# A decode block on one core: one ring of 160 KB for all loads, in which a load waits only for the readers of the bytes it replaces

## The chip, the cores and the metric

One Trainium2 chip, one of its cores. The metric is device microseconds of one execution, as the median of the fast runs; lower is better. A profile is one such execution with the hardware profiler on; its span is the time between its first and last instruction, and the time of a run is about 1.8 us longer than its span.

## The reference

One decode step of a transformer block, for a batch of 2, with one new token each:

```python
mod = (silu(c) @ w_mod)                    # w_mod 1024 x 6144: six vectors sa, ca, ga, sb, cb, gb
h = layernorm(x) * (1 + ca) + sa
q = h @ wq                                 # 32 heads of 128, 4 key/value heads, 8 query heads share one
p = softmax(q k_cache^T / sqrt(128))       # caches: 2 x 4 x 32768 x 128 each
x = x + ga * (p v_cache) @ wo
h = layernorm(x) * (1 + cb) + sb
x = x + gb * (gelu(layernorm(h) @ w1 + b1) @ w2 + b2)   # w1 1024 x 3584, w2 3584 x 1024
```

All inputs are bf16. K and V are 134.2 MB, the weights 44.0 MB, and each byte is used once for at most 8 query heads: 178.27 MB must come from HBM.

## The kernel before

All loads go out from SP, in one fixed order, into six slots of 16 KB per partition ("ring") and two fixed regions of 32 KB for `wo` and most of `w1`. A load waits for the readers of its slot, and for the load that landed in it last. A K or V chunk is 8192 rows: 16 KB per partition, 2 MB.

```python
seq = [Item("WMODH", 0, nslots=2)] + [Item("WQ", k) for k in range(KT8)]
seq += kv("K", 0) + kv("K", 1) + kv("V", 0)                     # kv: four chunks each
seq += [Item("MODB", 0), Item("MODB", 1)] + kv("K", 2) + kv("V", 1)
# ... (MODB: 1 MB in a slot of 2 MB; WO quarters go to the fixed regions)
seq += kv("K", 7) + kv("V", 6)
seq += [Item("W1", k, fixed="AB") for k in range(4)] + kv("V", 7) + [Item("W1", k, fixed="AB") for k in range(4, 6)]
seq += [Item("W1", k) for k in range(6, KT8)] + [Item("W2", j) for j in range(4)]
# ...
        if it.kind == "WO":                                      # rows of 2 KB
            return A_wo[r0:r0 + 512, :].rearrange("(t p) n -> p t n", p=128)
        if it.kind == "W2":                                      # rows of 2 KB
            return B_w2[it.i * 896:(it.i + 1) * 896, :].rearrange("(k p) n -> p k n", p=128)
```

Per (batch, group) `i` the engines do a whole K pass (64 PE transposes and 64 score matmuls a chunk, eight at a time, the transposed keys copied out of PSUM by DVE or ACT), then a whole V pass for the group before:

```python
    for i in range(1, NBG):
        QK(i)
        softmax_m1(i)
        softmax_back(i - 1)
        # ... (MODB)
        PV(i - 1)                 # per chunk 64 matmuls of 8 columns, V as stationary operand
        # ... (WO_mm: 256 matmuls of one column per batch)
        softmax_aux(i)            # maximum, then eight exponentials on ACT
    # ... last PV, WO, layernorm, W1, GELU, W2, store
```

It leaves out the second of the reference's last two layernorms; the changed kernel has it.

Of the kernel before, what the change touches and what calls it, by code (L numbers as in the profile page):

```python
# [5 lines left out]
ACT = mybir.ActivationFunctionType  # L6
# [6 lines left out]
HQ = 32  # L13
# [6 lines left out]
CH_ROWS = 8192  # L20
TPC = CH_ROWS // 128
NCH = S // CH_ROWS
# [6 lines left out]
R = 6  # L29
NKT = 8  # L30
PIPE = 3
NPKT = 4
NPS = 1
EVAC_PATTERN = ("dve", "act", "dve", "act", "dve", "dve", "act", "dve")
SLOT_BYTES = 16 * 1024


class Tracker:
# [115 lines left out]
    def dma(self, E, fn, key, reads=(), writes=()):  # L154
        self.dma_key(key)
        reads, writes = self._excl(reads, writes)
        waits = self._compute_waits(E, self._dep_tokens(E, reads, writes))
        self.dma_cnt[key] += 16
        token = (key, ("g", len(self.dma_groups[key])))
        self.ops[E].append(("dma", waits, fn, key))  # L160
        self._record(token, reads, writes)
        return token
# [34 lines left out]
def bass_adaLN_cond__gqa_block_cached__mixer_channel_mlp__decode_kernel(  # L197
# [17 lines left out]
    ident = nc.alloc_sbuf_tensor("ident", [128, 128], BF16)  # L215
    identf = nc.alloc_sbuf_tensor("identf", [128, 128], FP32)
    onesf = nc.alloc_sbuf_tensor("onesf", [128, 128], FP32)
    x16 = nc.alloc_sbuf_tensor("x16", [16, 128], BF16)
    c16 = nc.alloc_sbuf_tensor("c16", [16, 128], BF16)
    b1m = nc.alloc_sbuf_tensor("b1m", [FT, 128], BF16)  # L220
    b2m = nc.alloc_sbuf_tensor("b2m", [KT8, 128], BF16)
    smallT = nc.alloc_sbuf_tensor("smallT", [128, 68], FP32)
    xT = smallT[:, 0:16].rearrange("p (b k) -> p b k", b=2)
    cT = smallT[:, 16:32].rearrange("p (b k) -> p b k", b=2)
    b1T = smallT[:, 32:60]
    b2T = smallT[:, 60:68]
    sgT = nc.alloc_sbuf_tensor("sgT", [128, 2, KT8], FP32)
    siluT = nc.alloc_sbuf_tensor("siluT", [128, 2, KT8], BF16)
    stat = nc.alloc_sbuf_tensor("stat", [128, 8], FP32)
    mean = nc.alloc_sbuf_tensor("mean", [128, 2], FP32)  # L230
    rstd = nc.alloc_sbuf_tensor("rstd", [128, 2], FP32)
    xc = nc.alloc_sbuf_tensor("xc", [128, 2, KT8], FP32)
    sq = nc.alloc_sbuf_tensor("sq", [128, 2, KT8], FP32)
    t1 = nc.alloc_sbuf_tensor("t1", [128, 2, KT8], FP32)
    hT = nc.alloc_sbuf_tensor("hT", [128, 2, KT8], BF16)
    modT = nc.alloc_sbuf_tensor("modT", [128, NMOD, 2], FP32)
    qacc = nc.alloc_sbuf_tensor("qacc", [128, 2 * HQ], FP32)
    qT = nc.alloc_sbuf_tensor("qT", [128, 2, HQ], BF16)
    attnT = nc.alloc_sbuf_tensor("attnT", [128, 2, HQ], BF16)
    yT = nc.alloc_sbuf_tensor("yT", [128, 2, KT8], FP32)  # L240
    x1T = nc.alloc_sbuf_tensor("x1T", [128, 2, KT8], FP32)
    h2T = nc.alloc_sbuf_tensor("h2T", [128, 2, KT8], BF16)
    zT = nc.alloc_sbuf_tensor("zT", [128, FT, 2], FP32)
    z2 = nc.alloc_sbuf_tensor("z2", [128, FT, 2], FP32)
    z3 = nc.alloc_sbuf_tensor("z3", [128, FT, 2], FP32)
    th = nc.alloc_sbuf_tensor("th", [128, FT, 2], FP32)
    gT = nc.alloc_sbuf_tensor("gT", [128, FT, 2], BF16)
    mT = nc.alloc_sbuf_tensor("mT", [128, KT8, 2], FP32)
    resT = nc.alloc_sbuf_tensor("resT", [128, 2, KT8], FP32)
    res_bf = nc.alloc_sbuf_tensor("res_bf", [128, 16], BF16)  # L250
    res16 = nc.alloc_sbuf_tensor("res16", [16, 128], BF16)
    m1 = [nc.alloc_sbuf_tensor(f"m1_{i}", [128, HPG], FP32) for i in range(2)]
    gm = [nc.alloc_sbuf_tensor(f"gm_{i}", [HPG, 1], FP32) for i in range(2)]
    diag = [nc.alloc_sbuf_tensor(f"diag_{i}", [HPG, HPG], FP32) for i in range(2)]
    negm = [nc.alloc_sbuf_tensor(f"negm_{i}", [128, HPG], FP32) for i in range(2)]
    rowsum = [nc.alloc_sbuf_tensor(f"rowsum_{i}", [128, HPG], FP32) for i in range(2)]
    rinv = [nc.alloc_sbuf_tensor(f"rinv_{i}", [128, HPG], FP32) for i in range(2)]

    KB = 1024
    ARENA = R * SLOT_BYTES + 32 * KB + 32 * KB + 32 * KB  # L260
    arena = nc.alloc_sbuf_tensor("arena", [128, ARENA], mybir.dt.uint8)
    abase = nc.lookup_mloc(arena).addr

    def at(name, shape, dtype, off):
        return nc.alloc_sbuf_tensor_at(name, list(shape), dtype, offset=abase + off)

    def slot_off(sl):
        return sl * SLOT_BYTES

    slots = [at(f"slot{i}", [128, SLOT_BYTES // 2], BF16, slot_off(i)) for i in range(R)]  # L270
    regA = R * SLOT_BYTES
    regB = regA + 32 * KB
    regC = regB + 32 * KB
    wo_blk = [at("wo0", [128, 16, DM], BF16, regA), at("wo1", [128, 16, DM], BF16, regB)]
    w1p = [at(f"w1p{k}", [128, F], BF16, (regA + k * 7 * KB) if k < 4 else (regB + (k - 4) * 7 * KB)) for k in range(6)]
    for i in range(2):
        for q in range(4):
            T.interval(f"wo{i}q{q}", (regA if i == 0 else regB) + q * 8 * KB, (regA if i == 0 else regB) + (q + 1) * 8 * KB)
    for k in range(6):
        off = (regA + k * 7 * KB) if k < 4 else (regB + (k - 4) * 7 * KB)  # L280
        T.interval(f"w1p{k}", off, off + 7 * KB)
    S_sb = at("S_sb", [128, HPG, NCH * TPC], FP32, regC)
    E_sb = [at(f"E_sb{i}", [128, HPG, NCH * TPC], BF16, regC + 8 * KB + i * 4 * KB) for i in range(2)]
    KT_sb = [at(f"KT_sb{i}", [128, 8, 128], BF16, regC + 16 * KB + i * 2 * KB) for i in range(NKT)]
    assert 16 + 2 * NKT <= 32

    psKT = [nc.alloc_psum_tensor(f"psKT{i}", [128, 1024], BF16) for i in range(NPKT)]
    psS = [nc.alloc_psum_tensor(f"psS{i}", [128, 512], FP32) for i in range(NPS)]
    psO = nc.alloc_psum_tensor("psO", [128, 512], FP32)
    psM = nc.alloc_psum_tensor("psM", [128, 512], FP32)  # L290
    psX = nc.alloc_psum_tensor("psX", [128, 512], FP32)

    T.inst("pool", lambda e: e.memset(ident[:, :], 0.0), writes=["ident"])
    T.inst("pool", lambda e: e.affine_select(out=ident[:, :], in_=ident[:, :], compare_op=ALU.not_equal, fill=1.0,
                                             base=0, pattern=[[-1, 128]], channel_multiplier=1), reads=["ident"], writes=["ident"])
    T.inst("pool", lambda e: e.memset(identf[:, :], 0.0), writes=["identf"])
    T.inst("pool", lambda e: e.affine_select(out=identf[:, :], in_=identf[:, :], compare_op=ALU.not_equal, fill=1.0,
                                             base=0, pattern=[[-1, 128]], channel_multiplier=1), reads=["identf"], writes=["identf"])
    T.inst("pool", lambda e: e.memset(onesf[:, :], 1.0), writes=["onesf"])

    T.dma("act", lambda e: e.dma_start(x16[:, :], A_x.rearrange("b o (k p) -> (b o k) p", p=128)), key="ld", writes=["x16"])
    T.dma("act", lambda e: e.dma_start(c16[:, :], c.rearrange("b (k p) -> (b k) p", p=128)), key="ld", writes=["c16"])
    T.dma("act", lambda e: e.dma_start(b1m[:, :], B_b1.rearrange("(f p) -> f p", p=128)), key="ld", writes=["b1m"])
    T.dma("act", lambda e: e.dma_start(b2m[:, :], B_b2.rearrange("(f p) -> f p", p=128)), key="ld", writes=["b2m"])

    class Item:
        def __init__(self, kind, i=0, cc=0, nslots=1, fixed=None):
            self.kind, self.i, self.cc, self.nslots, self.fixed = kind, i, cc, nslots, fixed
            self.pos = None
            self.view = None  # L310
            self.regions = None
            self.issued = False

    def kv(kind, i):
        return [Item(kind, i, cc) for cc in range(NCH)]

    def woq(i, qs):
        return [Item("WO", i, q, fixed="AB") for q in qs]
    K4 = kv("K", 4)
    V3 = kv("V", 3)  # L320
    seq = [Item("WMODH", 0, nslots=2)] + [Item("WQ", k) for k in range(KT8)]
    seq += kv("K", 0) + kv("K", 1) + kv("V", 0)
    seq += [Item("MODB", 0), Item("MODB", 1)] + kv("K", 2) + kv("V", 1)
    seq += [Item("MODB", 2), Item("MODB", 3)] + kv("K", 3) + kv("V", 2)
    seq += [Item("MODB", 4), Item("MODB", 5)] + woq(0, [0, 1]) + K4[0:2] + woq(0, [2, 3]) + K4[2:4]
    seq += [Item("MODB", 6), Item("MODB", 7)] + woq(1, [0, 1]) + V3[0:2] + woq(1, [2, 3]) + V3[2:4]
    seq += kv("K", 5) + kv("V", 4)
    seq += kv("K", 6) + kv("V", 5)
    seq += kv("K", 7) + kv("V", 6)
    seq += [Item("W1", k, fixed="AB") for k in range(4)] + kv("V", 7) + [Item("W1", k, fixed="AB") for k in range(4, 6)]  # L330
    seq += [Item("W1", k) for k in range(6, KT8)] + [Item("W2", j) for j in range(4)]
    lookup = {}
# [405 lines left out]
```

## Time and profile before

| | before |
|---|---|
| time, median of 3 runs | 448.21 us (446.92 to 448.82) |
| span of the profile | 445.5 us |
| PE, ACT, DVE busy | 69%, 32%, 35% |
| bytes from HBM, mean rate | 178.28 MB, 400 GB/s over the span |

These lines are from the page of the kernel before. They give the busy tenths of the 16 DMA engines, and what they moved, in 40 slices of 11.1 us; then two DMA queues (loads, and instruction fetches): packets, MB, time taken as a share of 16 engines; then the chain of work that ended last, by engine.

```profile
DMA  8999999999999999999999999999999999999990
GB/s 316 421 425 433 419 423 431 420 344 424 425 430 420 427 427 419 414 413 410 417 413 403 428 425 430 422 384 415 430 424 418 427 382 383 427 425 414 394 369 34
...
q1 hardware_dynamic: 21616, 178.27, 96.7%
q8 instruction: 61, 1.00, 0.9%
...
PE 52%; DMA 19%; issue 11%; ACT 9%; SPq 6%; DVE 3%; ACTq 0%; DVEq 0%
```

The DMA engines are busy nearly everywhere, so the load stream is near its limit, yet several slices move clearly less than the 425 to 433 of the best. And the chain that ended last is mostly PE, with 11% of "issue", which is time in which an engine waited for nothing that the profile shows. In order of time, the last load in this chain, and the piece after it (start, us, what):

```profile
239.86 18.71 DMA slot_54<-in_A_v_cache_dram
258.62 1.89 PE psO L595 x64
```

Up to 258.6 us PE (106 us) and the loads (84 us) take turns in the chain. After that no load is in it: of its last 187 us, 125 are PE, 33 "issue" and 18 ACT. So the stream was not the limit from end to end. In the last part the computation ended last, and the loads waited for it to free their slots.

The next view is the busy time by stretch (microseconds from the start of the span; the last two columns are the share of the DMA engines and the rate):

```profile
core 0: us, PE busy (x) PEld busy (x) DVE busy (x) ACT busy (x) POOL busy (x), PEclk, DMA share, GB/s
30.00:88.00 58.00, 44.87 (x957) 43.34 (x958) 28.36 (x44) 26.80 (x41) 0.00 (x0) 0.94 1.01 426
88.00:104.00 16.00, 12.76 (x378) 12.32 (x376) 6.55 (x9) 5.07 (x6) 0.00 (x0) 0.86 0.94 368
184.00:248.00 64.00, 37.95 (x910) 35.97 (x906) 19.07 (x32) 16.89 (x30) 0.00 (x0) 0.69 1.02 411
...
360.00:378.00 18.00, 16.24 (x372) 16.01 (x370) 10.97 (x17) 10.79 (x19) 0.00 (x0) 0.93 0.94 373
408.00:430.00 22.00, 13.77 (x460) 13.32 (x457) 3.73 (x22) 1.76 (x3) 0.00 (x0) 0.50 1.03 396
```

There are two kinds of loss. In 88 to 104 and 360 to 378 the DMA engines are partly idle (shares 0.94): holes. In 184 to 248 and 408 to 430 they are fully busy and slow: these are the stretches of `wo` and `w2`, read in rows of 2 KB. Compared with 427 GB/s I work out, from the rates of each microsecond, 5.9 us lost in holes (2.2 in 88 to 104, 1.4 in 288 to 306, 2.2 in 360 to 378) and 3.9 in the slow stretches (2.4 and 1.5).

What SP waited for (us in total, times, longest), then PE's longest "issue" entry (time in which an engine waited for nothing that the profile shows):

```profile
SPq L184 <- PE psKT L540: 194.6, 28, 18.0
SPq L184 <- PE psO L595: 77.3, 24, 9.8
...
PE psO L595 <- issue: 23.8, 12, 2.6
```

```profile
82.87 0.33 SPq L396 DMA_DIRECT2D slot_52<-in_A_v_cache_dram  x1
88.67 0.33 SPq L396 DMA_DIRECT2D modb_83<-in_w_mod_dram  x1
94.46 0.33 SPq L396 DMA_DIRECT2D modb_84<-in_w_mod_dram  x1
97.60 0.33 SPq L396 DMA_DIRECT2D slot_49<-in_A_k_cache_dram  x1
```

SP issues whenever PE has read a slot out, once in 5.8 us in a K pass. At 427 GB/s (my estimate from the rate above) a full slot of 2 MB takes 4.9 us to load, but in 88.67 and 94.46 the next item of the fixed order is `modb`, 1 MB: half a slot, 2.5 us of work for the DMA engines each.

PE's "issue" gaps come above all in PV. Often PE runs 128 of its matmuls, which with their weight loads are 256 instructions, in 3.6 us, and then stands still for 2.3 to 2.6 us. Two of these gaps begin at 140.4 and 146.3, as a fetch of 16 KB of instructions starts (140.3 and 146.4), and end 1.3 to 1.5 us after its 1.05 us. It looks as if PE waited for its next instructions, but no run tests that.

At the end, PE's timeline (start, us, instruction, count, idle before and what ended it):

```profile
434.13 1.15 PE L689 MATMUL psM<-gT,w2v_93 128*128 128x2 bf16 x38 [1.97 <-DVE mT L680]
...
440.14 1.63 PE L689 MATMUL psX<-gT,w2v_96 128*128 128x2 bf16 x56
443.09 0.28 PE L699 MATMUL psM<-ident,res_bf 128*16 128x128 bf16 x1 [1.32 <-DVE res_bf L698]
```

The 224 matmuls of `w2` start at 434.1, when GELU is done, and run until 441.8.

### The profile page before, as it was taken

To read this page: it belongs to the slowest core of one execution; us is meant where nothing else is said; L and a number is where in the kernel's file an instruction comes from. 1 tells how busy PE (TensorE), PEld (TensorE's weight loads), DVE (VectorE), ACT (ScalarE), POOL (GpSimd) and SP (SyncE) were. 2 spreads that over 40 slices of the span, in tenths; PEclk is the share of its full clock that TensorE was granted. 3 is DMA by queue.
4 is the path that set the end of the run, shared out by engine and by line. 5 is a ranking of instruction groups with operands and counts; after the bars stand their busy time and mean duration, and the time that the engine had idled before them with its cause. 6 is when DMAs were issued, how large, how long until landed. Compare 5 with 4: busy or idle time off the path is not lost.

```text
span 445.5 us, 16705 instructions
## 1 busy us (share of the span) xinstructions
PE 309.0 (69%) x7805; PEld 295.2 (66%) x7805; DVE 157.9 (35%) x294; ACT 143.3 (32%) x251; POOL 1.3 (0%) x9
## 2 busy tenths in 40 slices
PE   1445987996986698638684258887977698755555
PEld 1445877895986598638574158886976588744455
DVE  1101656551652265215351004551643065400221
ACT  2001556630751166024250004640752065305100
POOL 1000000000000000000000000000000000000000
PEclk9999996995996599657696555995896579855555
DMA  8999999999999999999999999999999999999990
GB/s 316 421 425 433 419 423 431 420 344 424 425 430 420 427 427 419 414 413 410 417 413 403 428 425 430 422 384 415 430 424 418 427 382 383 427 425 414 394 369 34
DMA packets 21807, 179.35 MB, mean 403 GB/s; under 512 B 1770, under 2 KB 1770, under 8 KB 11498
## 3 DMA queue, kind: packets, MB, share of 16 engines
q1 hardware_dynamic: 21616, 178.27, 96.7%
q8 instruction: 61, 1.00, 0.9%
q14 instruction: 8, 0.07, 0.0%
q10 hardware_dynamic: 122, 0.02, 0.0%
HBM read 178.28 MB, written 0.00 MB: 400 GB/s over the span
## 4 chain that ended last, share of the span: by engine, by line
PE 52%; DMA 19%; issue 11%; ACT 9%; SPq 6%; DVE 3%; ACTq 0%; DVEq 0%
PE psKT L540 23%; PE psO L595 10%; DMA slot_53<-in_A_k_cache_dram 10%; PE psS L520 8%; SPq L396 5%; DMA wqv_77<-in_A_wq_dram 5%; DMA slot_54<-in_A_v_cache_dram 4%; PE psM L607 3%; ACT KT_sb_67 L550 3%; ACT S_sb L525 3%; ACT KT_sb_72 L550 2%; ACT E_sb_65 L576 1%; PE psM L572 1%; PE psM L478 1%; PE psM L567 1%
## 5 line engine op out<-in xcount | busy, mean ns | idle before, releaser
L550 ACT ACTIVATE KT_sb_72<-psKT 128x1024 bf16<-128x1024 bf16 x32 | 32.7, 1023 | 44.7 <-PE psKT L540 44.7
L550 ACT ACTIVATE KT_sb_67<-psKT 128x1024 bf16<-128x1024 bf16 x25 | 25.6, 1024 | 58.1 <-PE psKT L540 58.1
L576 ACT ACTIVATE E_sb_64<-S_sb,negm 128x256 bf16<-128x256 f32 x32 | 16.2, 506 | 78.1 <-DVE negm L574 77.3
L540 PE MATMUL psKT<-ident,slot_53 128*128 128x128 bf16 x384 | 35.5, 255 | 8.2 <-DMA slot_53<-in_A_k_cache_dram 8.2
L576 ACT ACTIVATE E_sb_65<-S_sb,negm 128x256 bf16<-128x256 f32 x32 | 16.2, 506 | 61.8 <-DVE negm L574 61.0
L553 DVE COPY KT_sb_70<-psKT 128x1024 bf16<-128x1024 bf16 x32 | 22.1, 692 | 36.2 <-PE psKT L540 36.2
L540 PEld LDWEIGHTS psKT<-ident,slot_53 128*128 128x128 bf16 x384 | 28.7, 116 | 8.4 <-DMA slot_53<-in_A_k_cache_dram 8.3
L540 PE MATMUL psKT<-ident,slot_51 128*128 128x128 bf16 x320 | 28.5, 251 | 4.7 <-DMA slot_51<-in_A_k_cache_dram 4.7
L540 PE MATMUL psKT<-ident,slot_54 128*128 128x128 bf16 x384 | 29.3, 218 | 1.2 <-issue 1.2
L598 DVE TENSOR_TENSOR attnT<-psO,rinv 128x8 bf16<-128x8 f32 x8 | 1.3, 167 | 79.2 <-PE psO L595 79.2
L553 DVE COPY KT_sb_66<-psKT 128x1024 bf16<-128x1024 bf16 x32 | 22.1, 692 | 19.6 <-PE psKT L540 19.4
L553 DVE COPY KT_sb_73<-psKT 128x1024 bf16<-128x1024 bf16 x32 | 22.1, 692 | 19.3 <-PE psKT L540 19.3
L553 DVE COPY KT_sb_68<-psKT 128x1024 bf16<-128x1024 bf16 x32 | 22.1, 692 | 17.9 <-PE psKT L540 17.9
L540 PE MATMUL psKT<-ident,slot_49 128*128 128x128 bf16 x320 | 27.0, 240 | 1.3 <-issue 1.3
L540 PEld LDWEIGHTS psKT<-ident,slot_51 128*128 128x128 bf16 x320 | 23.3, 114 | 5.4 <-DMA slot_51<-in_A_k_cache_dram 4.8
L550 ACT ACTIVATE KT_sb_69<-psKT 128x1024 bf16<-128x1024 bf16 x25 | 25.7, 1028 | 3.3 <-PE psKT L540 3.3
L540 PE MATMUL psKT<-ident,slot_50 128*128 128x128 bf16 x320 | 24.4, 218 | 0.3 <-issue 0.3
L540 PE MATMUL psKT<-ident,slot_52 128*128 128x128 bf16 x320 | 24.3, 218 | 0.0
L540 PEld LDWEIGHTS psKT<-ident,slot_49 128*128 128x128 bf16 x320 | 21.6, 108 | 1.4 <-issue 1.4
L553 DVE COPY KT_sb_71<-psKT 128x1024 bf16<-128x1024 bf16 x32 | 22.1, 691 | 1.0 <-PE psKT L540 0.8
L540 PEld LDWEIGHTS psKT<-ident,slot_54 128*128 128x128 bf16 x384 | 21.8, 97 | 0.0
L525 ACT ACTIVATE S_sb<-psS 128x512 f32<-128x512 f32 x32 | 19.0, 593 | 7.9 <-PE psS L520 7.9
(195 smaller groups left out, 517.1 us busy)
## 6 DMA issues: line engine op xcount, KB each, us to landing
slot_53<-in_A_k_cache_dram SPq DMA_DIRECT2D x6, 2048.0 KB, 15.6
slot_54<-in_A_k_cache_dram SPq DMA_DIRECT2D x6, 2048.0 KB, 17.6
slot_51<-in_A_v_cache_dram SPq DMA_DIRECT2D x6, 2048.0 KB, 17.1
slot_52<-in_A_v_cache_dram SPq DMA_DIRECT2D x6, 2048.0 KB, 19.8
slot_49<-in_A_k_cache_dram SPq DMA_DIRECT2D x5, 2048.0 KB, 17.1
slot_50<-in_A_k_cache_dram SPq DMA_DIRECT2D x5, 2048.0 KB, 20.3
slot_51<-in_A_k_cache_dram SPq DMA_DIRECT2D x5, 2048.0 KB, 19.2
slot_52<-in_A_k_cache_dram SPq DMA_DIRECT2D x5, 2048.0 KB, 19.2
```

What stands on the lines that cost most here:

```text
L396: T.dma("sp", lambda e, dst=dst, src=src: e.dma_start(dst, src), key=key, writes=list(it.regions))
L478: T.inst("pe", lambda e, jc=jc: e.matmul(psM[:, 288 + jc * 2:290 + jc * 2], lhsT=wv[:, jc * 128:(jc + 1) * 128], rhs=siluT[:, :, kb], star ...
L520: T.inst("pe", lambda e, sbk=sbk, sp=sp, kn=kn, jj=jj: e.matmul(psS[sbk][:, sp * HPG:(sp + 1) * HPG], lhsT=KT_sb[kn][:, jj, :], rhs=qT[:, ...
L525: T.inst("act", lambda e, sbk=sbk, col0=col0: e.activation(S_sb[:, :, col0:col0 + 64], psS[sbk][:, 0:512].rearrange("p (t h) -> p h t", h= ...
L540: T.inst("pe", lambda e, kq=kq, jj=jj, sl_view=sl_view, t=t: e.transpose(psKT[kq][:, jj * 128:(jj + 1) * 128], sl_view[:, t * 128:(t + 1) ...
L550: T.inst("act", lambda e, kq=kq, kn=kn: e.activation(KT_sb[kn][:, :, :], psKT[kq][:, 0:1024].rearrange("p (a n) -> p a n", a=8), ACT.Copy) ...
L553: T.inst("dve", lambda e, kq=kq, kn=kn: e.tensor_copy(KT_sb[kn][:, :, :], psKT[kq][:, 0:1024].rearrange("p (a n) -> p a n", a=8)), reads=[ ...
L567: T.inst("pe", lambda e: e.matmul(psM[0:HPG, 0:128], lhsT=m1[j][:, :], rhs=identf[:, :], start=True, stop=True), reads=[f"m1_{j}", "identf ...
L572: T.inst("pe", lambda e: e.matmul(psM[:, 128:128 + HPG], lhsT=onesf[0:HPG, :], rhs=diag[j][:, :], start=True, stop=True), reads=["onesf", ...
L576: T.inst("act", lambda e, h=h: e.activation(E_sb[j][:, h, :], S_sb[:, h, :], ACT.Exp, bias=negm[j][:, h:h + 1], scale=SCALE, accum_out=row ...
L595: T.inst("pe", lambda e, t=t, sl_view=sl_view, tg=tg: e.matmul(psO[:, 0:HPG], lhsT=sl_view[:, t * 128:(t + 1) * 128], rhs=E_sb[j][:, :, tg ...
L607: T.inst("pe", lambda e, wv=wv, t=t, cch=cch: e.matmul(psM[:, col0 + cch:col0 + cch + 1], lhsT=wv[:, t % 16, cch * 128:(cch + 1) * 128], r ...
```

## The change

One ring of 160 KB per partition for everything. Every load has its own semaphore and waits for one thing, the PE count at which the readers of the bytes under it are done. K chunk n alternates with V chunk n-5. `w_mod` comes whole at the start, in rows of 12 KB, and no longer in half filled slots between the caches. `w1` and `w2` come last (before, four of the eight blocks of `w1` came ahead of the last V pass), `wo` and `w2` are laid out so that rows are 16 KB and 8 KB. PV takes E as the stationary operand (32 columns) and 512 columns of V as the moving one, four matmuls to four column groups; so 16 instead of 64 per chunk. The maximum is taken per chunk, S is double-buffered as E already was, and the softmax steps are put between the groups of the next K chunk. The core of the diff:

```diff
-R = 6
-NKT = 8
+VLAG = 5
+NKT = 6
+RING = 160 * 1024
-SLOT_BYTES = 16 * 1024
@@ class Tracker
-    def dma(self, E, fn, key, reads=(), writes=()):
+    def dma(self, E, fn, key, reads=(), writes=(), frees=()):
         self.dma_key(key)
         reads, writes = self._excl(reads, writes)
-        waits = self._compute_waits(E, self._dep_tokens(E, reads, writes))
+        tokens = self._dep_tokens(E, reads, writes)
+        for r in frees:
+            reg = self._region(r)
+            assert reg[1], r
+            tokens.extend(reg[1])
+        waits = self._compute_waits(E, tokens)
@@ stream (the old slots, regions and seq are gone; cut)
+    for n in range(NK + VLAG):
+        if n < NK:
+            add(("K", n), [TPC, D], kv_src(A_k_cache, n // NCH, n % NCH))
+        v = n - VLAG
+        if v >= 0:
+            add(("V", v), [TPC, D], kv_src(A_v_cache, v // NCH, v % NCH))
+            if v % (2 * NCH) == 2 * NCH - 1:
+                g = v // (2 * NCH)
+                add(("wo", g), [8, DM], A_wo[g * 1024:(g + 1) * 1024, :].rearrange("(p j) n -> p j n", j=8))
+    # (then w1 in 4 items, w2 in 4 items)
+    w2_v = B_w2.rearrange("(q p j) n -> p q (j n)", p=128, j=4)
+    def need(*key):
+        it = by_key[key]
+        while pos[0] <= it.n:
+            cur = stream[pos[0]]
+            old = [o.reg for o in stream[:cur.n] if o.off < cur.off + cur.nbytes and cur.off < o.off + o.nbytes]
+            # ... dst, the view of cur
+            T.dma("sp", lambda e, dst=dst, src=cur.src: e.dma_start(dst, src), key=f"d_{cur.reg}", writes=[cur.reg], frees=old)
+            pos[0] += 1
+        return it
@@ PV
-            for t in range(TPC):
-                tg = cc * TPC + t
-                T.inst("pe", ... matmul(psO[:, 0:HPG], lhsT=sl_view[:, t * 128:(t + 1) * 128], rhs=E_sb[j][:, :, tg], ...
+        for t4 in range(TPC // 4):
+            tg = cc * TPC + t4 * 4
+            q = t4 % 4
+            pe(... matmul(psO[32 * q:32 * q + 32, :], lhsT=E_sb[j][:, tg // 4, :, :].rearrange("p h t -> p (h t)"),
+                          rhs=it.view[:, t4 * 4:t4 * 4 + 4, :].rearrange("p t d -> p (t d)"), ...
```

The intent: no load waits for anything but free space, PE may fall far behind before the stream stops, and the tail of the computation runs while the last weights load.

## The prediction

> **What bounds the kernel now.** The load stream. The page counts 178.27 MB on the SP queue; the 16 DMA engines are busy 96.7% of a 445.5 us span for it, at a mean 403 GB/s; PE is busy 69%, ACT 32%, DVE 35%. In the busy table by 11 us stretches, undisturbed K and V stretches move 422 to 430 GB/s. [...]no stretch passes 434. At 425 the bytes alone take 419.5 us. So 26 us of the span can be won at most:
> - start: first bytes at 2.3 us (kept);
> - holes: 262 GB/s at 93-96 us, 336 at 99-102, 306 to 393 at 363-375, a dip at 297-308. SP waits for slots with unread K or V (waits of the SP queue: 195 us on transposes, 77 on PV). By subtraction about 9 us of stream time;
> - short rows: w2 and wo are read in 2 KB runs and move at 386 to 400 GB/s with the DMA engines fully busy. For 15.7 MB that costs about 3.4 us against 425;
> - tail: the last byte lands near 434.3 us. Of the 11 us after it 8 are the w2 product (224 small matmuls that begin only after GELU, at 434, with an issue gap), 3.7 the closing chain and store.
>
> **What the change does.** Six 16 KB slots plus fixed regions become one ring of 160 KB, ten chunks. A load waits for one PE count, the readers of the chunk ten places earlier. A chunk takes 4.9 us at 425 GB/s, so PE may fall some 35 us behind before the stream stops; before, about 20, with whole K passes alternating with whole V passes, where now K n and V n-5 alternate. wo and w2 rows become 16 and 8 KB. PV turns from 64 matmuls of 8 columns per chunk into 16 of 512 columns in four column groups. The tail gains a layernorm (about 3.5 us in the chain of waits).
>
> **Does PE keep up?** In the timeline a K chunk with its scores takes 5.8 us at full clock. PV is estimated: 8192 columns, against 8 transposes of 128 columns in 0.5 us, so at most 3.9 us if the four groups run serially, about 1 if they overlap. Together 6.8 to 9.7 us per step, against 9.9 us of loading. ACT (3 evictions of 1.02, a score copy of 0.59, two exponentials of 0.5) needs about 5 us, DVE about 4.5. The stream stays the limit, narrowly if PV serialises.
>
> **Tail.** After the last V chunk, wo, w1 and w2 (16.8 MB, 39 us) still stream, and fit in the ring. Last PV, extraction, wo, two layernorms, w1 and GELU take about 27 us, so they hide; 32 matmuls (about 1 us) and the closing chain of 3.7 us follow the last byte. That saves about 6 us.
>
> **Sum.** Span: 2.3 start + 1 ramp + 418 (426 GB/s) + 5 tail = 426; timed runs exceed the span by 2.7 us: **429 us**, range 424 to 437. Chances: faster by over 2% 0.91, within 2% 0.08, slower 0.01.
>
> **What would show it.** DMA row at 9 in every slice, at least 420 GB/s through K/V and over w2; SP's waits for PE remaining but harmless; last byte about 5 us before the end; PE waiting for K and V chunks; w1 done before w2 lands.
>
> **What would make it wrong.** PV serial at a low granted clock, so that PE needs over 9.9 us per step (PE busy above 9 tenths, DMA holes between chunks); softmax stalls longer than the ring covers; w1 starting late, so w2 queues behind it; more loads outstanding slowing each other below 420 GB/s.

The sum: 2.3 + 1 + 418 + 5 is 426, and with 2.7 it is 429. The 426 GB/s in it are from the stretches of the kernel before (422 to 430).

## More of the kernel before

From the trace's record of arriving semaphore increments, the last load landed at 436.9. So 8.6 us of the span came after the last byte. But `w2` did not wait for it: its matmuls waited for GELU, whose chain is the computation since 258.6.

## The result, and the profile after

| | before | after |
|---|---|---|
| time, median of 4 runs each | 447.56 us (445.39 to 448.82) | 431.44 us (431.30 to 431.47) |
| span of the profile | 445.5 us | 429.7 us |
| last byte landed | 436.9 us | 425.7 us |
| from there to the end | 8.6 us | 4.0 us |
| instruction fetches of 16 KB | 61 | 47 |

The ratio is 0.9642 (95% interval 0.9604 to 0.9680). Ratios here are the mean time of one kernel's fast runs over the mean of the other's of the same rounds, so not quite the ratio of the medians. The change saves 15.8 us of span: the last byte lands 11.2 us earlier (436.9 less 425.7), and 4.6 us less follow it. For the kernel before this split is bookkeeping, as its end did not wait for its last byte.

The same lines of the page of the changed kernel, with one more ahead of them, the busy us of the engines (share of the span, number of instructions):

```profile
PE 292.2 (68%) x6035; PEld 258.2 (60%) x6035; DVE 162.5 (38%) x344; ACT 158.9 (37%) x266; POOL 1.3 (0%) x9
...
DMA  8999999999999999999999999999999999999992
GB/s 332 432 422 426 433 432 424 432 424 427 427 432 427 426 433 429 427 433 426 426 432 426 430 433 424 429 432 426 429 429 428 430 429 424 435 424 424 427 386 112
...
q1 hardware_dynamic: 14112, 178.27, 97.6%
q8 instruction: 47, 0.77, 0.6%
...
DMA 70%; PE 24%; ACT 2%; DVE 2%; issue 1%; SPq 1%; ACTq 0%
```

From the second slice to the second but last no slice is under 420 GB/s, and the chain that ended last is now 70% DMA, where it was 52% PE. The stretches shown above for the kernel before, here in the changed kernel:

```profile
30.00:88.00 58.00, 38.15 (x948) 37.06 (x948) 19.91 (x35) 15.86 (x18) 0.00 (x0) 1.00 1.01 427
88.00:104.00 16.00, 10.99 (x218) 10.02 (x219) 5.89 (x13) 11.14 (x23) 0.00 (x0) 0.89 1.01 429
184.00:248.00 64.00, 49.71 (x973) 43.48 (x970) 30.68 (x57) 32.25 (x57) 0.00 (x0) 0.89 1.01 429
...
360.00:378.00 18.00, 9.84 (x128) 4.91 (x124) 5.39 (x17) 7.71 (x19) 0.00 (x0) 0.70 1.00 427
408.00:430.00 22.00, 9.83 (x312) 9.23 (x311) 1.55 (x7) 0.25 (x1) 0.00 (x0) 0.50 0.59 247
```

The K/V stage runs at 427 to 431 GB/s. What SP waited for:

```profile
SPq L344 <- PE psS L441: 197.4, 31, 11.3
SPq L344 <- PE psM L510: 47.1, 3, 16.3
SPq L344 <- PE psO L473: 36.1, 27, 8.0
```

SP still waits 281 us for PE in these three lines, where it was 272 in the two before. That means nothing by itself: it waits with up to ten loads in flight (K and V loads land 43 to 44 us after their issue, by the page), and the DMA queue is not empty meanwhile. The wait of SP, which runs ahead, is not a loss here: the DMA row stays at 9 tenths from the second slice to the last but one.

A step of PE at full clock (the last group of a K chunk, the 16 PV matmuls, and the next K chunk), from the timeline:

```profile
307.44 0.34 PE L441 MATMUL psS<-qT,KT_sb 128*128 128x8 bf16 x8
307.72 1.05 PE L473 MATMUL psO<-V,E_sb 128*32 128x512 bf16 x16
312.09 0.62 PE L546 MATMUL psKT<-ident,K 128*128 128x128 bf16 x8 [3.33 <-DMA K<-in_A_k_cache_dram]
```

PV takes 1.0 us, then PE sits idle for 3.3 us until the next K chunk lands. (At full clock a step is 6.2 us, eight groups of 0.65 us and PV. At lower clock it is longer: in 184 to 248, at a mean granted clock of 0.89, PE was busy for 49.7 of 64 us.) The tail:

```profile
423.31 1.87 PE L591 MATMUL psS<-gT,w 128*128 128x2 bf16 x64 [3.28 <-DMA w<-in_B_w_dram]
425.74 1.01 PE L591 MATMUL psS<-gT,w 128*128 128x2 bf16 x32 [0.56 <-DMA w<-in_B_w_dram]
427.28 0.28 PE L597 MATMUL psM<-ident,res_bf 128*16 128x128 bf16 x1 [0.53 <-DVE res_bf L596]
```

`w2` is now used as it lands, and only 32 matmuls and the closing chain come after the last byte at 425.7.

One stretch does not fit: 408 to 430 moves only 247 GB/s. Reading it by the microsecond, the DMA share is 1.0 until 416, and from 418 to 424 it is 0.4 to 0.5: as if half of the DMA engines had nothing left while the other half still work. The trace records when each of the 16 increments of a load's semaphore arrived, but not from which of the 16 DMA engines. I read them as one from each engine, which fits the DMA share (0.5 from 419 to 420, when 8 of the last load's 16 have arrived). I print some loads of the changed kernel, in us:

```
load of               first   8th    9th    last   spread
wmod, 5th              21.1   21.3   21.4   21.5    0.4
wmod, 6th              24.8   25.0   25.0   26.3    1.6
a chunk near  88       85.7   86.1   87.2   88.7    3.0
a chunk near 148      144.1  145.2  147.0  148.5    4.4
a chunk near 218      212.2  214.3  216.4  218.0    5.8
a chunk near 287      280.2  282.2  285.9  287.5    7.3
a chunk near 361      353.2  356.0  360.2  361.8    8.6
w2, the last          416.7  419.5  423.7  425.7    9.0
```

PE takes up the last load with its last increment (425.74 in the timeline above, for 425.7), so the stream ends when the latest engine ends: 425.7, where the first was done at 416.7. The spread hardly creeps, it jumps by 1.1 to 1.3 us at six loads, the ones shown first landing late at 26.3, 88.7, 148.5, 218.0, 287.5 and 361.8. The instruction fetches number 1, 9, 17, 25, 33 and 41 start at 21.3, 86.3, 142.4, 214.9, 285.0 and 356.9. So the spread grows once in eight fetches, just after a fetch. That is a theory to test: fetches of 16 KB (one packet each, 0.94 us in the mean of 47) fall in turn on the same eight engines and make these late.

### The profile page after: what moved, and what is told of

The parts are those of the page before. It is cut to its first block, busy times and chain, and to the rows that moved or that the text cites. A ratio compares the mean times of both kernels' runs of the same rounds, so it can differ in the third digit from the quotient of the medians.

```text
span 429.7 us, 12974 instructions
## 1 busy us (share of the span) xinstructions
PE 292.2 (68%) x6035; PEld 258.2 (60%) x6035; DVE 162.5 (38%) x344; ACT 158.9 (37%) x266; POOL 1.3 (0%) x9
## 4 chain that ended last, share of the span: by engine, by line
DMA 70%; PE 24%; ACT 2%; DVE 2%; issue 1%; SPq 1%; ACTq 0%
DMA K<-in_A_k_cache_dram 50%; PE psKT L546 15%; DMA V<-in_A_v_cache_dram 9%; DMA w<-in_B_w_dram 7%; DMA wmod<-in_w_mod_dram 5%; PE psS L441 4%; PE psO L473 2%; PE psM L510 1%; ACT E_sb L462 1%; SPq L344 1%; PE psM L494 0%; DVE KT_sb L552 0%; PE psM L483 0%; ACT L462 0%; DVE msum L488 0%
## 5 line engine op out<-in xcount | busy, mean ns | idle before, releaser
L546 PE MATMUL psKT<-ident,K 128*128 128x128 bf16 x2048 | 181.1, 240 | 55.1 <-DMA K<-in_A_k_cache_dram 54.2
L546 PEld LDWEIGHTS psKT<-ident,K 128*128 128x128 bf16 x2048 | 138.2, 108 | 70.0 <-DMA K<-in_A_k_cache_dram 63.5
L550 ACT ACTIVATE KT_sb<-psKT 128x1024 bf16<-128x1024 bf16 x96 | 98.3, 1024 | 190.2 <-PE psKT L546 181.3
L552 DVE COPY KT_sb<-psKT 128x1024 bf16<-128x1024 bf16 x160 | 108.2, 689 | 137.7 <-PE psKT L546 137.0
L441 PE MATMUL psS<-qT,KT_sb 128*128 128x8 bf16 x2048 | 91.6, 168 | 7.2 <-ACT KT_sb L550 4.5
L441 PEld LDWEIGHTS psS<-qT,KT_sb 128*128 128x128 bf16 x2048 | 84.0, 100 | 8.6 <-ACT KT_sb L550 4.9
L473 PE MATMUL psO<-V,E_sb 128*32 128x512 bf16 x512 | 38.2, 424 | 10.1 <-DMA V<-in_A_v_cache_dram 9.5
L462 ACT ACTIVATE E_sb<-S_sb,negm 128x256 bf16<-128x256 f32 x64 | 32.5, 508 | 7.0 <-DVE negm L460 5.2
L447 DVE TENSOR_REDUCE m1c<-S_sb 128x8 f32<-128x512 f32 x32 | 22.0, 688 | 14.1 <-ACT S_sb L446 13.0
L418 PE MATMUL psS<-siluT,wmod 128*128 128x2 bf16 x384 | 11.2, 165 | 8.4 <-DMA wmod<-in_w_mod_dram 6.9
L462 ACT ACTIVATION_READ_ACCUMULATOR E_sb<-S_sb,negm 128x1 f32 x64 | 12.0, 187 | 0.0
```

The costliest lines, as they stand in the source:

```text
L418: pe(lambda e, w=it.view, j=j, k=k: e.matmul(psS[0][:, 2 * j:2 * j + 2], lhsT=w[:, j * 128:(j + 1) * 128], rhs=siluT[:, :, k], start=(k == ...
L441: pe(lambda e, t=t, jj=jj: e.matmul(ps[:, t * HPG:(t + 1) * HPG], lhsT=KT_sb[kn][:, jj, :], rhs=qT[:, b, g * HPG:(g + 1) * HPG], start=Tru ...
L447: dve(lambda e: e.tensor_reduce(m1c[:, :, cc], Sc, AX.X, ALU.max), reads=[f"S_sb{i % 2}_{cc}"], writes=[f"m1c{cc}"])
L462: act(lambda e, h=h: e.activation(E_sb[j][:, :, h, :], S_sb[j][:, h, :].rearrange("p (u t) -> p u t", t=4), ACT.Exp, bias=negm[j][:, h:h + ...
L473: pe(lambda e, t4=t4, tg=tg, q=q: e.matmul(psO[32 * q:32 * q + 32, :], lhsT=E_sb[j][:, tg // 4, :, :].rearrange("p h t -> p (h t)"), rhs=i ...
L546: pe(lambda e, kq=kq, jj=jj, w=it.view, t=t: e.transpose(psKT[kq][:, jj * 128:(jj + 1) * 128], w[:, t, :], ident[:, :]), reads=[it.reg, "i ...
```

## The experiments

All of the changed kernel unless "before" is in the name. All passed the comparison with the reference, the four with a result wrong on purpose too, so it does not notice these errors. Beside them the kernel before measured 447.70, 447.56 and 446.82 us in the three sets of runs.

### What closed the holes: depth or order?

ring6 makes the ring as deep as the six slots were. blocks brings back whole K passes and whole V passes, in loading and in use. blocks_ring6 does both.

```diff
-RING = 160 * 1024
+RING = 96 * 1024                      # ring6, blocks_ring6
-VLAG = 5
+VLAG = 4                              # blocks, blocks_ring6; the same loop in place of pv(n - VLAG)
-        v = n - VLAG
-        if v >= 0:
+        for v in range(n - NCH + 1 - VLAG, n + 1 - VLAG) if n % NCH == NCH - 1 and n > NCH else ():
             add(("V", v), ...
```

> The changed kernel with a ring of 96 KB, six chunks, as deep as the slots before. Theory A (alternating K n with V n-5 is what closed the holes, six chunks are enough because PE needs about 7 us of every 9.9): 431 to 434 us, GB/s above 420 in every slice of the K/V stage. Rival B (the depth closed the holes): 437 us or more, slices under 410 GB/s.

> The changed kernel, ring of ten chunks, but whole K passes of four chunks alternate with whole V passes of four, as before the change, in loading and in use. Theory A (the alternation closed the holes): 435 us or more, holes again at the start of K or V passes. Rival B (the depth did, ten chunks cover a pass either way): 431 to 433 us, no holes.

> Both undone: whole passes and six chunks. Both theories: the holes come back, 436 to 443 us, slices of 300 to 410 GB/s. If it stays below 433 us then neither depth nor order closed the holes, and the shorter PE and ACT work per step did.

Measured: 431.37, 431.33 and 431.96 us (431.21 to 432.32). Neither alone costs anything, and both together about half a microsecond. So both of my theories fall: the ring's depth and the alternation were not what brought the time. The rates of blocks_ring6 by slice, from its page:

```profile
GB/s 334 429 423 424 432 432 423 429 425 431 431 428 425 432 428 429 431 423 413 424 430 431 429 426 432 420 394 425 432 428 428 432 426 414 392 430 421 428 423 154
```

Some slices do fall to 392 to 394, so holes come back with six chunks and whole passes, but the last byte lands at 426.5 instead of 425.7. The landings hint at why a hole is nearly free here: the last load's spread is 4.9 us instead of 9.0. My reading, as the trace does not tell the engines apart: when the stream stops for a moment, the engines that were ahead have nothing to do, and the late ones, which set the end, are still working off their queue. My expectation for this run had named the third possibility, that shorter work per step closed the holes of the kernel before. The record fits it: before, four V chunks took PE 9 to 12 us with the gaps of "issue", and now they take about 4 at full clock; and in blocks_ring6 the chain that ended last again has loads in it up to 426.5. But no run gave the changed kernel back the 64 PV matmuls per chunk or the old softmax, so this is argued, not shown.

### Holes and rows in the kernel before

before_mended is the kernel before with `wo` and `w2` in long rows (rows permuted, so wrong), with the 1 MB items of `w_mod` paired to fill a slot. Four items of `wq` are paired too, to keep the slots' numbering.

```diff
-seq += [Item("MODB", 0), Item("MODB", 1)] + kv("K", 2) + kv("V", 1)    # and so for the three others
+seq += [Item("MODB", 0)] + kv("K", 2) + kv("V", 1)
-            return A_wo[r0:r0 + 512, :].rearrange("(t p) n -> p t n", p=128)
+            return A_wo[r0:r0 + 512, :].rearrange("(p t) n -> p t n", p=128)
-            return B_w2[it.i * 896:(it.i + 1) * 896, :].rearrange("(k p) n -> p k n", p=128)
+            return B_w2[it.i * 896:(it.i + 1) * 896, :].rearrange("(p k) n -> p k n", p=128)
```

> The kernel before, with wo and w2 read in long rows (which permutes them, result wrong on purpose) and with the 1 MB loads of w_mod packed in pairs into a 16 KB slot. Theory (short rows and half filled slots are two of the stream's losses before, 2.4 us in 184-248, 2.2 us in 408-434, 2.2 us in the hole at 88-104; the holes near 297 and 366 come from PE work between passes and stay; the tail is a chain of compute after the last V, so the w2 rate does not matter): 4 to 5 us less than before, 442 to 444.5; the stretch 88-104 at 420 or more. Rival (the hole at 88-104 has another cause): it stays below 400 there.

Measured: 443.68 us (442.07 to 444.98), ratio 0.9926 (0.9900 to 0.9952), 3.1 us less by the medians where I had expected 4 to 5. A first build that paired only `w_mod` shifted the order of issue, so that a `w1` load overwrote `wo` before its last use. The stretches:

```profile
88.00:104.00 16.00, 11.92 (x356) 11.48 (x354) 6.34 (x8) 4.29 (x6) 0.00 (x0) 0.81 1.01 422
184.00:248.00 64.00, 39.83 (x962) 37.77 (x958) 19.18 (x32) 16.90 (x30) 0.00 (x0) 0.66 1.01 423
...
360.00:378.00 18.00, 15.16 (x371) 14.72 (x368) 9.25 (x15) 10.25 (x12) 0.00 (x0) 1.00 0.98 393
```

The hole at 88 to 104 is gone (368 to 422 GB/s), so half filled slots made it. The stretch of `wo` rises from 411 to 423. The hole at 360 to 378 stays in part (373 to 393). I put it down to PE work between the passes that frees no slot (there, in the kernel before, two loads of SP are 14.8 us apart, 349.5 and 364.3, with gaps of "issue", `wo` and softmax in between), but no run took that work out alone: argued, not shown. That the gain is small fits the chain: its last load lands at 255.4 instead of 258.6, 3.2 us earlier, and no load is in the chain after that here either.

short_rows is the changed kernel with `wo` and `w2` in rows of 2 KB again (wrong).

```diff
-A_wo[g * 1024:(g + 1) * 1024, :].rearrange("(p j) n -> p j n", j=8)
+A_wo[g * 1024:(g + 1) * 1024, :].rearrange("(j p) n -> p j n", j=8)
-    w2_v = B_w2.rearrange("(q p j) n -> p q (j n)", p=128, j=4)
+    w2_v = B_w2.rearrange("(t p) n -> p t n", p=128)      # item k takes w2_v[:, 4 * lo:4 * hi, :]
```

> The changed kernel with wo and w2 read in 2 KB runs again, as before the change (result wrong on purpose: the rows land in other places). Theory (short rows cost stream time at the DMA engines): wo and w2 stretches at 386 to 405 GB/s, 3 to 4 us more, 434.3 to 435.5 us. Rival (the low rate before came from something else in those stretches, such as cold PE work): rate stays at 424 or more and the time at 431.4.

Measured: 433.92 us, 2.5 us more. The theory holds: packets of 2 KB took 86 ns of an engine and those of 16 KB 614 ns, by my count in the trace, which is 382 and 427 GB/s for 16 engines (in the kernel before those of 2 KB took 88 ns, and its `w2` moved at 388 GB/s from 415 to 433). The size is smaller than the 3 to 4 us I expected, because the time is that of the latest landing. The mean of the 16 landings of the last load moved by 3.4 us (421.2 to 424.6), the latest only by 2.4 (425.7 to 428.1).

### Does PE keep up, and by how much?

pv_serial sends all 16 PV matmuls of a chunk to one column group (wrong). PSUM is set to zero first, as the other rows are still read.

```diff
-matmul(psO[32 * q:32 * q + 32, :], ... start=(cc == 0 and t4 < 4), stop=(cc == NCH - 1 and t4 >= TPC // 4 - 4)
+matmul(psO[0:32, :], ... start=(cc == 0 and t4 < 1), stop=(cc == NCH - 1 and t4 >= TPC // 4 - 1)
```

> All 16 PV matmuls of a chunk go to one column group instead of four (result wrong on purpose, same number of instructions and loads). In the changed kernel 16 take 0.98 us, so the four groups overlap; in one group I expect 3.4 to 3.6 us at full clock. Theory (PE has slack under the stream): PE busy rises by 60 to 90 us and the time stays within 431 to 434 us. Rival (the column groups are what lets PE keep up): a step passes 9.9 us, holes appear, 437 us or more.

Measured: 432.42 us (431.36 to 432.55), 1.0 us more. Its timeline at a step, then from its page the busy us and the rates by slice:

```profile
308.39 0.34 PE L442 MATMUL psS<-qT,KT_sb 128*128 128x8 bf16 x8
308.66 3.63 PE L474 MATMUL psO<-V,E_sb 128*32 128x512 bf16 x16
```

```profile
PE 352.6 (82%) x6035; PEld 275.3 (64%) x6035; DVE 160.9 (37%) x345; ACT 157.6 (37%) x266; POOL 1.3 (0%) x9
...
GB/s 329 435 421 425 430 435 426 423 431 429 429 426 429 432 426 426 434 432 418 432 431 426 428 434 429 424 429 431 428 428 428 433 423 429 435 424 422 429 364 92
```

PV takes 3.63 us instead of about 1, and PE is busy 352.6 us instead of 292.2, yet the stream hardly feels it. The column groups give PE much slack, but they are not what made the kernel faster. (This run keeps the 16 long matmuls per chunk, with 6.3 us of "issue", so it says nothing about the 64 short ones before.)

### The tail

weights_early moves `w1` and `w2` ahead of the last V chunk and the last `wo`.

```diff
+        if v == NK - 1:
+            # add w1 (4 items) and w2 (4 items) here instead of after the loop
         if v >= 0:
             add(("V", v), ...
```

> The changed kernel with w1 and w2 loaded just ahead of the last V chunk and the last wo, instead of after them (same bytes, same ring). Theory (loading w1 and w2 last hides the tail of attention, layernorms, w1 and GELU behind 34 us of loading): the stream ends at about 425 as now, and then about 26 to 33 us of tail stand open: 450 to 462 us. If the tail were cheap either way: below 440 us.

Measured: 456.21 us, slower than the kernel before (ratio 1.0188, 1.0161 to 1.0216). PE's busy tenths and the rates by slice, from its page:

```profile
PE   0634389869787739867676787697749953000566
...
GB/s 340 428 424 425 436 425 431 426 423 434 423 430 431 428 427 431 430 428 429 427 427 430 431 428 424 431 428 428 433 425 424 433 428 419 430 427 367 69 3 3
```

The bytes end at 425.5, as in the changed kernel, and then 29 us of PE, DVE and ACT work stand open. So loading in the order that hides this work is worth 24.8 us (456.21 less 431.44), more than the whole change. It is not a part of the change's gain, though: the kernel before, too, loaded `w2` and half of `w1` last.

### The wait in the title

landing_waits adds to each load the wait for the landing of what it replaces.

```diff
             tokens.extend(reg[1])
+            tokens.append(reg[0])
         waits = self._compute_waits(E, tokens)
```

> The changed kernel, with each load into the ring waiting also for the landing of the loads whose bytes it replaces, beside their readers. Theory (a reader has itself waited for the landing, so nothing is added but a wait instruction on SP): 431.2 to 431.6 us. Rival (the narrower wait in the title is worth time): 433 us or more.

Measured: 431.34 us. Waiting for the readers alone is worth nothing here, as a reader has itself waited for the landing.

### Why the last engine is late

more_pe adds 64 one-column matmuls to each of the 32 K steps. half_scores leaves out half of the transposes and score matmuls from the third chunk on (wrong).

```diff
+        if n < NK:                                             # more_pe
+            for r in range(64):
+                pe(lambda e: e.matmul(psM[0:1, 480:481], lhsT=ident[:, 0:1], rhs=ident[:, 0:1], start=True, stop=True), ...
-        for jj in range(8):                                    # half_scores, at both places
+        for jj in (range(8) if n < 2 else (0, 2, 4, 7)):
```

> The changed kernel with 64 one-column matmuls more in each of the 32 K steps (4096 more PE instructions with their weight loads, no more data, PE has room). Theory C (instruction fetches of 16 KB, each near 0.95 us on one DMA engine, fall on about half of the engines and make these late; the last byte comes from the latest): 16 fetches more, 63 instead of 47, spread of the 16 landings of the last load up from 9.0 us to about 12, time up by 2.5 to 3.5 us to 434 to 435. Rival D (some engines are simply slower in moving data): fetches rise but the spread stays near 9 us and the time at 431.4 to 432.

> The changed kernel with only 4 of every 8 transposes and score matmuls from the third K chunk on (result wrong on purpose; same loads, evictions and waits; 3840 PE instructions fewer). Theory C (each round of 8 instruction fetches puts about 1.4 us on the 8 late engines): 32 fetches instead of 47, the steps in the landing spread come once in 8 fetches and so more rarely, the last load's spread falls from 9.0 to about 6 us, the last byte comes near 423, time 428 to 429.3. Rival D (the late engines are slow at moving data, whatever PE does): last byte at 425.7, time 431.2 to 431.5.

Lines of PE and of the fetch queue, of more_pe and then of half_scores:

```profile
PE 350.1 (79%) x8083; PEld 315.5 (71%) x8083; DVE 162.7 (37%) x344; ACT 159.9 (36%) x266; POOL 1.3 (0%) x9
...
q8 instruction: 63, 1.03, 0.8%
```

```profile
PE 249.8 (59%) x4115; PEld 197.2 (46%) x4115; DVE 157.9 (37%) x344; ACT 156.4 (37%) x266; POOL 1.3 (0%) x9
...
q8 instruction: 32, 0.52, 0.4%
```

more_pe measured 444.41 us, far over either expectation. Its last byte landed at 428.2, 2.5 us later than in the changed kernel; but PE had fallen behind (busy 350 us) and then needed 14 us for a tail that no loading hid any longer. So its time says nothing about the fetches. half_scores measured 428.59 us, where theory C had said 428 to 429.3 and the rival 431.2 to 431.5: its last byte landed at 422.8, with a spread of 6.2 us. The first of the 16 landings of the last load stayed where it was, at 416.7: only the late landings moved. And in all three the jumps of the spread follow the fetches:

```
kernel        fetches  of them number 1, 9, 17, 25, ... start at                 spread jumps by 1.1 to 1.6 us at a load that lands at
changed          47    21.3  86.3 142.4 214.9 285.0 356.9                        26.3  88.7 148.5 218.0 287.5 361.8
more_pe          63    21.0  86.4 137.7 189.0 239.6 290.3 339.1 390.3            23.0  88.9 143.8 193.8 243.9 293.9 344.0 394.0
half_scores      32    21.5  88.2 205.8 326.4                                    26.5  93.7 211.9 330.0
```

The kernels issue instructions at different paces, and the jumps go with the count of fetches, not with time or bytes. And 4096 PE instructions more (weight loads counted) gave 16 fetches more, 3840 fewer gave 15 fewer: 256 a fetch. That speaks for theory C. (Which engine a fetch ran on the trace does not tell: that it is the eight late ones is inferred. A jump, 1.1 to 1.6 us, is more than the 0.94 us of a fetch; why stays open. In more_pe the spread also falls twice, by 2 to 3 us, when the stream stopped for PE.)

### Two tries to even the engines out

The aim was to put the last load on the early engines. last_on_8 cuts the last 1 MB of `w2` into 16 loads of 8 partitions, on my assumption that each of them runs on the same 8 engines; pool_last issues these from POOL, each after a tiny load of 8 partitions, on my assumption that they then fall on the other 8. (The trace doesn't number the engines, so no run here shows either.)

```diff
+            if cur is stream[-1]:
+                for s in range(16):
+                    lo, hi = 8 * s, 8 * s + 8
+                    # pool_last: first a load of 8 x 8 elements, and "pool" for "sp"
+                    T.dma("sp", lambda e, lo=lo, hi=hi, cur=cur: e.dma_start(cur.view[lo:hi, :, :], cur.src[lo:hi, :, :]), ...
```

> The changed kernel with its last load (1 MB of w2) cut into 16 loads of 8 partitions[...]. Theory E (the 8 engines that finish early, at 417 to 419 us, are those 8): the last byte comes about 2.4 us earlier, at 423.3, time 429.0. Rival F (those 8 are the late ones): about 2.4 us later, 433.5 to 434.

> The changed kernel with its last load (1 MB of w2) issued from POOL as 16 loads of 8 partitions, each after a tiny load of 8 partitions[...]. Theory E2 (those are the early ones): last byte 423.2 to 424, time 428.8 to 430. If [...]they fall on the late ones: 433 to 438. If they spread over all 16: 431.4.

"Those 8" in theories E and F are the engines of such a load from SP, "those" in theory E2 are the 8 that last_on_8 did not use.

last_on_8 measured 437.52 us. Each of these loads shows 8 increments of data, where the others show 16; they land one after the other until 430.8. Neither theory fits. The load before them has eight landings by 418.3 and eight from 425.2 on. Of the 8 increments of the first small load, six arrive at 415.0 to 418.8 and two at 425.5 and 425.9, and so on to the last. So, by the times of its landings, such a load uses six early engines and two late ones, and waits for the two. The loss is 6 us, where rival F had 2.4; part of it comes sooner, as the load before them already lands 3.5 us later than in the changed kernel (426.8 for 423.3), which stays open. It also means that pool_last aimed at the wrong engines: if eight are late, six of them are among those that last_on_8 did not use. pool_last measured 446.32 us. The rates by slice and POOL's queue, from its page:

```profile
GB/s 338 425 427 424 434 425 432 428 424 431 428 425 432 431 426 428 434 431 422 425 437 428 428 428 428 432 426 432 426 424 434 429 425 428 407 309 289 319 308 19
...
q0 software_dynamic: 1024, 1.05, 0.9%
```

The whole stream, SP's and POOL's loads together, falls to 289 to 319 GB/s while POOL's 1 MB is in flight (these loads land between 388.8 and 420.1), though the page shows the DMA engines busy in 9 tenths or more. After that the rate is 414 again (420 to 425). Which engines POOL's loads fell on can't be told, and why they slow the stream by a quarter stays open. No version beat the changed kernel with a right result; half_scores, which is no answer, marks what 15 fetches fewer are worth.

## Why the prediction was right

- **What bounds it: right for the changed kernel, only in part for the one before.** The stream, at 427 to 431 GB/s through K/V where I had summed with 426. In the kernel before, loads and PE took turns up to 258.6 us; from there the computation was the limit, with 33 us of "issue" in the chain, which I had not read. I counted its holes and its tail as losses of the stream, and the sum did not suffer, as it is a sum for the kernel after.
- **PE keeps up: right.** PV took 1.0 us, my lower estimate, so the column groups overlap: the same 16 matmuls took 3.63 us in one group and 1.05 in four, 3.5 times. A step at full clock is 6.2 us of the 9.9 that loading takes.
- **Tail: right in mechanism, mis-sized.** I took the last byte before for 434.3, where the mean DMA share falls, but the latest engine landed at 436.9. So 4.6 us were saved after the last byte, not 6; and 4.0 us follow it now, not 5.
- **Rows: right.** 2.5 us of time in the changed kernel, for 3.4; in the mean of the engines it is the 3.4.
- **Holes: right that they would close, and the given reason failed.** I named the ring of ten chunks, and K n alternating with V n-5. With six chunks and whole passes the time was the same within 0.5 us. One hole before came from half filled slots (shown), the others I think from PE being late, with its gaps of "issue" and the work between passes (argued). That they closed by the change as a whole is measured; that I had it right for a wrong reason was luck.
- **The term of the sum that failed.** "2.3 start + 1 ramp + 418 (426 GB/s)" put the last byte at 421.3; it landed at 425.7. A mean rate over 16 engines can't tell the end of a stream: the mean of the 16 landings of the last load is 421.2, close to the sum, but the end is that of the latest landing, and eight of the 16 fall behind at the instruction fetches (by theory C because their engines carry these), 7.4 us in six jumps for the latest. The tail of 4.0 for 5 gave back 1.0, and the run exceeds its span by 1.8 us, not by the 2.7 I had taken from a profile and a median of different runs. 429 + 4.4 - 1.0 - 0.9 is 431.5, for 431.44 measured.

## What to carry to other kernels

When a load stream is the limit, read its end from the last landing of each load rather than from the mean DMA share, and ask what else the DMA engines carry; here instructions came in fetches of 16 KB, and 15 fewer were worth 2.9 us. Look in the chain for the last load before you call a stream the limit to the end: here it was at 258.6 of 445.5 us. Order the stream so that the loads which need no long computation after them come last: the other order cost 24.8 us, while the depth of the ring, from six chunks to ten, was worth nothing measurable. Fill each slot (the hole from half filled ones moved 368 GB/s, the same stretch 422 with full ones), and read long rows (`wo` and `w2` in rows of 2 KB cost 2.5 us).
